# Six more out-weight blocks decoded during the attention, and GpSimd's forms set aside during the first left sums

## The chip, the core and the metric

The kernel runs on one core of a Trainium2 chip. The core has TensorE (PE in the profile; PEld are its weight loads), VectorE (DVE), ScalarE (ACT), GpSimd (POOL) and SyncE (SP), which issues nearly all DMAs. Each engine works through its own queue in order and waits for others by semaphores. The metric is the device time of one execution in microseconds (us). Everything is fp32 except the routing of the attention.

## The reference

Two stages follow each other. The first is attention with routing: 4 batches x 8 heads, 768 positions, 64 dimensions per head, 16 centroids per head. The second is a feed-forward block on the 3072 tokens x 512 features that come out.

```python
q_n = q / (norm(q) + 1e-6); k_n, c_n likewise
q_assign = argmax(einsum('bhsd,hcd->bhsc', q_n, c_n)); k_assign likewise
scores = where(q_assign[..., None] == k_assign[..., None, :], q @ k.T / 8, -1e9)
attn   = exp(scores - max); attn = attn / (sum + 1e-9)
x      = (attn @ v) -> (B*S, H*D) = (3072, 512)

h   = x @ w_in                      # w_in 512 x 2048
sp  = softplus(h)
out = (h * erf(sp)) @ w_out         # w_out 2048 x 512
```

## The kernel before

**Attention.** Two heads make a pair; there are 16 pairs (`NPAIR`), and each pair has 12 units of work: two halves of the queries by six blocks of keys. A period, `period(p, i)` (line 1343), handles two units; a pair has six periods, i = 0 to 5. In a period TensorE computes the scores of its two units into PSUM (`products`, `scores`), ScalarE takes the exponential (`curve`, written to the tiles `pr`), GpSimd adds the exponentials up (`accumulate`, line 548, 128x768, written to `more_out`) and TensorE multiplies those of the period before with v (`attend`). At i = 0 and i = 3 a half is complete: `divide` (line 573) begins with a TensorE product of the accumulated sum with a constant tile, `turned<-more_out,minus` in the profile; it needs GpSimd's last sum of the half. Half a pair ahead of all this, `maxima_step` (line 461) lets TensorE compute the scores once more, in bf16, into the PSUM tile `wide`, and VectorE takes their maxima (`nmx<-wide`). There is one `wide`: TensorE writes it again when VectorE has read it.

**Decoding the weights.** The products of the feed-forward block run by fast matrix multiplication of Strassen's kind. Each weight is read from DRAM as 64-bit numbers and made into fp32 on the chip, in 32 blocks of 128x512 values: blocks 0 to 15 are w_in, 16 to 31 w_out. For one block: `fetch` (a DMA of 512 KB into a place), `size`, `rest` and `sign` on ScalarE, `bounded` and `shifted` on VectorE (tensor_scalar), `summed` on GpSimd (int32, 128x512), after which the place is refetched for a later block. The first `N_EARLY` = 32 - `N_LATE` blocks are done inside the attention, two per pair: block n1 = 2p - 1 mostly in periods 1 to 4 of pair p, block n2 = 2p from period 3 of pair p to period 1 of pair p + 1. They use five places: two halves each of the token buffers `x_of[0]` and `x_of[1]`, and a part of `x_more`. With `N_LATE` = 10 these are blocks 0 to 21, and the last is finished in pair 11. Token chunk 0 is loaded into `x_of[0]` behind pair 11 (`load_x(0)`, `LAST_X`).

**Forms.** Fast multiplication needs sums and differences of matrix blocks. `left_forms` of the weights and `right_forms` of the first tokens are made in the last pairs: the list `forms` is taken from in turn by VectorE (`FORMS` says how many in which period of which pair, line 1409) and by GpSimd (in the pairs of `POOL_FORMS`, at `i % HJ == 1`, that is in periods 1 and 4, line 1436). On GpSimd a form stands in the queue behind the accumulations of its period's call.

**The first feed-forward stages.** Tokens are worked on in chunks of 512. `hidden(0, 0)` and `hidden(0, 1)` are the two halves of the hidden layer of chunk 0: 28 steps each, where a step is four matmul instructions into one of eight PSUM banks, followed by one or two VectorE operations that empty the bank (`block`, line 726; the bank of step k is used again by step k + 8). Between steps, `block` issues side work from the list `aside_work`, `pace` items per step. `gates` is such work: ScalarE's Softplus and Erf of a finished quarter (128x2048), an idle stretch in the list, four VectorE products with the result, and four left sums (`add_hidden`) for the next multiplication. `weights(n)` (line 1541) is the decoding of a late block in five items; its last item also lets GpSimd make `MADE_BEFORE[n]` of the 18 forms of `forms_twice` (line 969) whose results go to DRAM from `x_of[1]` and another tile. `out_forms` are GpSimd's forms of w_out, four per group. `project(0, 0)` is the first part of the output product; its side work needs token chunk 1, which is loaded into `x_of[1]` (line 1586).

All order is program order: `InOrder` (line 126) keeps each engine's instructions as the program issues them. Its line 136 is the line of nearly every instruction in the profile, so instructions are told apart by tiles.

Of the kernel before, what the change touches and what calls it, by code (L numbers as in the profile page):

```python
# [28 lines left out]
HJ = NJ // 2  # L29
# [8 lines left out]
LC = 512  # L38

UP = 2.0**16  # L40
PLACES = 5
FORMS = {12: {0: 1}, 13: {0: 1}, 14: {0: 1, 3: 1}, 15: {0: 1, 3: 2, 4: 2, 5: 2}}
POOL_FORMS = range(12, 16)
BIG = 2.0**60
FLOOR = 2.0**50
EPS = 2.0**-70
NPT = NJ + 2
N_LATE = 10
LAST_X = 11
MASKS = {(0, 2): ("k", 0), (2, 0): ("q", 0), (2, 2): ("k", 1), (5, 2): ("q", 1)}  # L50
FIRST_MASKS = {(2, 0): ("k", 0), (2, 1): ("q", 0), (2, 2): ("k", 1), (5, 2): ("q", 1)}
# [63 lines left out]
WHERE = {"x": (0, 0), "u": (0, 1), "w": (1, 1)}  # L115
TWICE = 2
BY_VECTOR = 4
MADE_BEFORE = (3, 3, 1, 1, 0, 1, 3, 2, 0, 0)
LAST_AT = (3, 6, 9, 12, 15, 18, 21)
EARLY_OUTERS = 6  # L120
STORE_AFTER = 2
# [23 lines left out]
def kernel(  # L145
# [145 lines left out]
    for f in range(HF):  # L291
        for g in (f, HF + f):
            w_steps.append((w_out[:, g], moe_w_out[g * P : (g + 1) * P]))
    N_EARLY = len(w_steps) - N_LATE

    x_of = {n: xp.tile([P, DM // P, CT], F32, name="x_own") for n in range(2)}
    places = [x_of[n][:, i : i + 2].rearrange("p k t -> p (k t)") for n in range(2) for i in (0, 2)]
    places.append(x_more.rearrange("p a k t -> p (a k t)")[:, 0 : 2 * LC])
    place_of = {n: places[n % PLACES] for n in range(N_EARLY)}
    after_of = {n: n + PLACES for n in range(N_EARLY - PLACES)}  # L300
    steps = {}

    def fetch(n):
        t = place_of[n]
        queues[0].dma_start(out=t.bitcast(U32), in_=w_steps[n][1])
        words = t.rearrange("p (n w) -> p n w", w=2)
        steps[n] = words[:, :, 1], words[:, :, 0], t.bitcast(I16)[:, 1 : 4 * LC : 4]
# [8 lines left out]
    def size_and_rest(n):  # L316
        size(n)
        rest(n)
# [360 lines left out]
    g_of = {}  # L679
    sums_of = {}  # L680
# [9 lines left out]
    aside_work = []  # L690
# [68 lines left out]
    def gate(n, lot, s):  # L759

        g = g_of[n, s, lot].rearrange("p h j t -> p (h j t)")
        box = []

        def curves():
            t = actp.tile([P, 2 * FG * HT], F32, name="a_s")
            box.append(t)
            ae.activation(out=t, in_=g, func=ACT.Softplus)
            ae.activation(out=t, in_=t, func=ACT.Erf)

        def product(i):  # L770
            c = slice(i * 512, (i + 1) * 512)
            ve.tensor_tensor(out=g[:, c], in0=box[0][:, c], in1=g[:, c], op=ALU.mult)

        return curves, [functools.partial(product, i) for i in range(2 * FG * HT // 512)]
# [5 lines left out]
    def idle(n):  # L780
        return [lambda: None] * n

    def gates(n, lot, which=(0, 1), between=()):
        work = list(between)
        for s in which:
            curves, products_of = gate(n, lot, s)
            if s == which[0]:
                work = [curves] + work + idle(7 - len(work)) + products_of
            else:
                work += [curves, *sums, *idle(3)] + products_of  # L790
            sums = add_hidden(n, lot, s)
        return work + sums
# [531 lines left out]
    def run(work):  # L1324
        for _ in work:
            pass
# [10 lines left out]
    forms = []  # L1337
# [5 lines left out]
    def period(p, i):  # L1343
        u = 2 * NJ * p + 2 * i
        n1, n2 = 2 * p - 1, 2 * p
        early = lambda n: 0 <= n < N_EARLY

        def mask(place):
            which = (MASKS if p else FIRST_MASKS).get((i, place))
            if which:  # L1350
                return masks(p + 1, *which, turned[0 if i in (0, 5) else 1], place > 1, ve if i == 0 else ae)
            return lambda: None

        if u > 0:
            for which in turns if i in (0, 3) else ():
                turn(*which)
                turns.remove(which)
            step_ahead(u)
        mask(0)()
        next(part[0], None)  # L1360
        if i == 5:
            next(routing[0], None)
        if i == 0 and p:
            run(routing[0])
        if u == 2:
            next(routing[0])
        products(u)
        products(u + 1)
        mask(1)()
        second = step_ahead(u + 1, True) if u > 0 else iter(())  # L1370
        next(second, None)
        rows = D if u == 0 or u + NJ >= len(units) else Q
        scores(u, rows)
        next(second, None)
        if i:
            next(second, None)
        next(part[0], None)
        scores(u + 1, rows)
        later = mask(2)
        if i == 0:  # L1380
            later()
            later = lambda: None
            next(second, None)
        if i == 3:
            similarities(p + 2)
            routing[0] = choose(p + 2, sc_of[u + 1][:, 0], True)
        curve(u)
        later()
        curve(u + 1)
        if u == 0:  # L1390
            step_ahead(1)
            similarities(1)
            routing[0] = choose(1, turned[0])
            next(routing[0])
            next(routing[0])
            vectors(1, "q")
            vectors(1, "k")
        if i == 0 and early(n1 - 1):
            bounded(n1 - 1)
            shifted(n1 - 1)  # L1400
            sign(n1 - 1)
        elif i == 1 and early(n1):
            size_and_rest(n1)
        elif i == 3 and early(n1):
            bounded(n1)
            sign(n1)
        elif i == 5 and early(n2):
            rest(n2)
        for _ in range(min(len(forms), FORMS.get(p, {}).get(i, 0))):
            forms.pop(0)[0]()  # L1410
        if i == 3:
            next(routing[0], None)
            if early(n1):
                shifted(n1)
            for _ in range(2):
                next(routing[0], None)
        elif i == 1:
            load(p + 1, "v", v, vp)
            if p == 0:
                run(routing[0])  # L1420
                transposes(2, "q")
        elif i == 2:
            transposes(p + 2, "k")
        elif i == 4:
            vectors(p + 2, "k")
            vectors(p + 2, "q")
        elif i == 5:
            transposes(p + 3, "q")
        if u > 0:
            if i == 1 and early(n1 - 1):  # L1430
                summed(n1 - 1)
            elif i == 4 and early(n1):
                summed(n1)
            for w in (u - 2, u - 1):
                accumulate(w)
            if i % HJ == 1 and p in POOL_FORMS and forms:
                forms.pop(0)[1]()
            for w in (u - 2, u - 1):
                attend(w)
            if i % HJ == 0:  # L1440
                part[0] = divide(u - 1)
                next(part[0])
        if i == 3 and early(n2):
            size(n2)
# [43 lines left out]
        copy()  # L1488
    transposes(1, "q")
    load(0, "v", v, vp)  # L1490
    for n in range(PLACES - 1):
        fetch(n)
    for i in range(NJ):
        run(maxima_step(0, i, also if i % 2 else wide))
# [6 lines left out]
    turn(0, 0, (ae.copy, ve.tensor_copy))  # L1501
    turns.clear()
    transposes(1, "k")
    fetch(PLACES - 1)
    queues[0] = queues[1] = sy
    for p in range(NPAIR):
        for i in range(HJ * 2):
# [25 lines left out]

    places = [gsp.tile([P, 3, FG, P], F32, name="g_more").rearrange("p a j t -> p (a j t)") for _ in range(2)]
    places += [outp.tile([P, 2, DM], F32, name="osb").rearrange("p h m -> p (h m)") for _ in range(2)]
    place_of.update({N_EARLY + i: places[i % 4][:, 0 : 2 * LC] for i in range(N_LATE)})
    after_of.update({N_EARLY + i: N_EARLY + i + 4 for i in range(N_LATE - 4)})
    for i in range(4):
        fetch(N_EARLY + i)

    def weights(n):
# [4 lines left out]
    making = forms_twice(  # L1546
        GROUPS[1][1][:EARLY_OUTERS],
        (actp.tile([P, 2 * FG * HT], F32, name="a_s"), x_of[1].rearrange("p k t -> p (k t)")),
    )
# [4 lines left out]
    def summed_after_forms(n):  # L1554
        for _ in range(MADE_BEFORE[n - N_EARLY]):
            next(making, idle(1)[0])()
        summed(n)

    def all_weights(lo, hi):
        return sum((weights(n) for n in range(lo, hi)), [])  # L1560

    out_forms = [right_forms(ge, *w_out_parts(f, 2)) for f in range(0, HF, 2)]

    def fence():
        t = up.tile([P, HM], F32, name="u")
        g = g_of[1, 0, 0][:, 0, 0, 0:1]
        ge.tensor_tensor(out=t[:, 0:1], in0=g, in1=g, op=ALU.add)

    def together(a, b):
        work = []  # L1570
        while a or b:
            work += a[:1] + b[:1]
            del a[:1], b[:1]
        return work
# [1 line left out]
    aside_work += idle(3) + all_weights(0, 4) + out_forms[0] + out_forms[1]  # L1576
    hidden(0, 0, {0: finish_attention})
    finish_aside()
    aside_work += together(idle(2) + gates(0, 0, (0,)), all_weights(4, N_LATE))
    hidden(0, 1, pace=2, first=ve.tensor_copy)  # L1580
    finish_aside()
    for store in making:
# [4 lines left out]
    aside_work += gates(0, 0, (1,)) + gates(0, 1, (0,), right_forms(ve, *x_parts(1)))  # L1587
    project(0, 0, 3)
    finish_aside()
    aside_work += together(gates(0, 1, (1,)), idle(2) + [fence] + out_forms[3])  # L1590
    take_places(2)
    hidden(1, 0, first=ve.tensor_copy)
    finish_aside()
# [1 line left out]
    making = forms26(EARLY_FORMS)  # L1595
# [7 lines left out]
    making = forms26(LATE_FORMS)  # L1603
# [41 lines left out]
```

## Time and profile before

| what | value |
|---|---|
| median of three runs | 967.66 us (966.88 to 968.11) |
| the profiled execution, its own time | 967.78 us |
| its span, first to last instruction | 966.1 us |
| attention, first exponential of pair 0 to the last `attend` | 20.2 to 407.4 us |
| `hidden(0, 0)`, TensorE | 407.41 to 432.27 us |
| `hidden(0, 1)`, TensorE | 432.27 to 463.95 us |
| `project(0, 0)`, TensorE | from 463.95 us |
| GpSimd busy, slices 2 to 16 of 40 | 8 or 9 tenths |
| granted TensorE clock, mean | 0.997 |

A line of the timeline gives the start in us from the span's start, the duration, the engine, the line, the operation, the tiles written and read, the shape, how many such instructions are merged in the line, and in brackets the idle time of the engine before it with what ended it. Ends of matmuls are modelled and overlap the next start, so the pace of TensorE is read from start to start. A digit of a slice is the busy share in tenths of a 24.15 us slice, which happens to be nearly one pair.

### The profile page before, as it was taken

Reading aid. Unit: us, or ns where it says so; the run is one execution under the profiler, and the core shown is the slowest. Engines: PE = TensorE matmul, PEld = TensorE weight load, DVE = VectorE, ACT = ScalarE, POOL = GpSimd, SP = SyncE. Lnnn points to the kernel's source line nnn. Section 1 sums busy time; section 2 is a strip of 40 time slices with the busy share of each in tenths; the row PEclk is TensorE's granted clock in tenths of the full one; section 3 lists DMA queues with packets and bytes.
Section 4 is the critical chain, followed back from the end, with each engine's and each line's share of the span. In section 5 each row is a group of like instructions: output and inputs, shape, how many; then the busy total and the mean of one; then the engine's idle time right before and its main releaser. Section 6 shows DMA issues by size and latency. Waiting matters only on the chain.

```text
span 966.1 us, 22439 instructions
## 1 busy us (share of the span) xinstructions
PE 953.0 (99%) x8954; PEld 729.1 (75%) x8954; DVE 810.8 (84%) x1399; ACT 540.8 (56%) x815; POOL 536.7 (56%) x370
## 2 busy tenths in 40 slices
PE   8999999999999999998999999999999999999998
PEld 3555555555555555686888888998999899989987
DVE  8888888888888876889779889788968987896887
ACT  3777777777777665467523542544266235625541
POOL 1688888888888888899369910360044015202700
PEclk9999999999999999999999999999999999999999
DMA  9355444444434311083203445363445336343533
GB/s 219 64 111 111 111 111 110 111 111 111 89 68 106 72 35 35 18 287 123 100 1 153 156 141 151 127 202 114 160 121 172 113 131 208 109 142 122 155 118 110
DMA packets 172313, 116.06 MB, mean 120 GB/s; under 512 B 131376, under 2 KB 141104, under 8 KB 172208
## 3 DMA queue, kind: packets, MB, share of 16 engines
q1 hardware_dynamic: 169280, 113.41, 42.1%
q8 instruction: 71, 1.16, 0.5%
q10 hardware_dynamic: 2928, 1.21, 0.4%
q14 instruction: 34, 0.28, 0.1%
HBM read 90.21 MB, written 24.38 MB: 119 GB/s over the span
## 4 chain that ended last, share of the span: by engine, by line
PE 93%; DVE 3%; DMA 1%; ACT 1%; issue 1%; SPq 0%; DVEq 0%; ACTq 0%
PE bank L136 40%; PE turned L136 31%; PE sc L136 17%; PE wide L136 6%; DVE g L136 1%; DVE w_out L136 1%; DVE nmx L136 1%; DMA out_dram<-osb 0%; ACT a_s L136 0%; DMA in_k<-in_k_dram 0%; DVE osb L136 0%; SPq L136 0%; DMA in_q<-in_q_dram 0%; DVE kT L136 0%; ACT g_more L136 0%
## 5 line engine op out<-in xcount | busy, mean ns | idle before, releaser
L136 POOL TENSOR_TENSOR more_out<-more_out,pr 128x768 f32<-128x768 f32 x128 | 217.1, 1696 | 18.7 <-ACT pr L136 10.1
L136 DVE TENSOR_REDUCE nmx<-wide 128x2 f32<-128x768 f32 x189 | 180.5, 955 | 47.4 <-PE wide L136 46.8
L136 ACT ACTIVATE pr<-sc 128x768 f32<-128x768 f32 x192 | 148.7, 810 | 94.0 <-PE wide L136 77.2
L136 POOL TENSOR_TENSOR g<-g 128x512 f32<-128x512 f32 x36 | 47.1, 1309 | 217.5 <-DVE g L136 215.6
L136 PE MATMUL turned<-pr,in_v 128*32 128x193 f32 x3072 | 144.8, 330 | 0.0
L136 PEld LDWEIGHTS turned<-pr,in_v 128*32 128x32 f32 x3072 | 91.6, 110 | 50.7 <-issue 21.3
L136 PE MATMUL sc<-qT,kT 64*128 64x384 f32 x528 | 98.4, 486 | 0.0
L136 DVE TENSOR_TENSOR g<-g 128x512 f32<-128x512 f32 x114 | 79.9, 700 | 16.4 <-PE bank L136 12.9
L136 DVE TENSOR_TENSOR g<-a_s,g 128x512 f32<-128x512 f32 x80 | 75.3, 966 | 4.2 <-ACT a_s L136 4.2
L136 POOL TENSOR_TENSOR more_out<-pr,pr 128x768 f32<-128x768 f32 x32 | 60.4, 1887 | 27.9 <-ACT pr L136 27.9
L136 PE MATMUL bank<-w_out,g 128*128 128x256 f32 x328 | 75.7, 380 | 0.0
L136 DVE TENSOR_TENSOR g<-bank,g 128x256 f32<-128x256 f32 (+1 forms) x129 | 63.7, 522 | 13.1 <-PE bank L136 5.9
L136 ACT ACTIVATE a_s<-g 128x1024 f32<-128x1024 f32 (+1 forms) x36 | 41.0, 1149 | 60.0 <-POOL g L136 45.6
L136 PE MATMUL bank<-x_own,w_in 128*128 128x128 f32 (+1 forms) x432 | 72.0, 309 | 2.3 <-DVE g L136 2.3
L136 PE MATMUL bank<-g_more,g 128*128 128x256 f32 x304 | 71.8, 379 | 0.0
L136 PEld LDWEIGHTS bank<-w_out,g 128*128 128x128 f32 x328 | 62.1, 190 | 9.6 <-issue 1.4
L136 PEld LDWEIGHTS <-qv 64*128 64x128 bf16 x384 | 26.9, 93 | 52.8 <-issue 36.7
L136 PEld LDWEIGHTS bank<-x_own,w_in 128*128 128x128 f32 x432 | 60.9, 192 | 7.0 <-DVE g L136 3.1
L136 PEld LDWEIGHTS sc<-qT,kT 64*128 64x128 f32 x528 | 49.6, 187 | 21.7 <-ACT inv L136 2.7
L136 PE MATMUL wide<-kv,qv 64*128 64x384 bf16 x378 | 64.0, 328 | 1.1 <-ACT km L136 0.6
L136 PEld LDWEIGHTS bank<-g_more,g 128*128 128x128 f32 x304 | 57.8, 190 | 7.8
L136 PE MATMUL wide<-km,qm 64*128 64x384 bf16 (+1 forms) x378 | 62.6, 327 | 0.0
(243 smaller groups left out, 2066.6 us busy)
## 6 DMA issues: line engine op xcount, KB each, us to landing
g_more<-b_dram SPq DMA_DIRECT2D x48, 512.0 KB, 3.6
g_more<-w_dram SPq DMA_DIRECT2D x84, 256.0 KB, 2.8
x_own<-in_moe_w_in_dram SPq DMA_DIRECT2D x13, 512.0 KB, 5.5
in_v<-in_v_dram SPq DMA_DIRECT2D x32, 192.0 KB, 3.1
x_dram<-more_out SPq DMA_DIRECT2D x128, 48.0 KB, 1.7
x_own<-x_dram SPq DMA_DIRECT2D x6, 1024.0 KB, 5.5
in_k<-in_k_dram SPq DMA_DIRECT2D x59, 96.0 KB, 2.7
in_q<-in_q_dram SPq DMA_DIRECT2D x58, 96.0 KB, 4.8
```

The source lines that it names most:

```text
L136: ins = getattr(self.engine, name)(*args, **kw)
```

## The change

- `N_LATE` goes from 10 to 4: blocks 22 to 27 (w_out) are decoded in the attention as well, in pairs 11 to 14. Their places follow `PLACE_OF`: blocks 0 to 24 go round the five places as before, and blocks 25, 26 and 27 use the two places in `x_of[1]`, where no token chunk is loaded yet.
- GpSimd's forms of the attention are taken in pairs 8 to 15, one per pair at period 4, instead of two per pair in pairs 12 to 15 at periods 1 and 4. Their number is the same, eight.
- In `hidden(0, 0)` the late blocks are now 28 to 31, and three forms of `forms_twice` stand between them instead of eight.
- In `hidden(0, 1)` the six blocks are gone from the side work. Since they were interleaved with the gate's items and the pace stays at two, the gate's items now go two to a step. Behind the four left sums GpSimd gets a one-column operation (`fence`) that reads the last of them; then come eight forms of `forms_twice`. Three more follow after the stage.

TensorE's order of instructions is the same.

```diff
-PLACES = 5
-POOL_FORMS = range(12, 16)
+POOL_FORMS = range(8, 16)
-N_LATE = 10
+N_LATE = 4
+PLACE_OF = [n % 5 for n in range(25)] + [2, 3, 2]
...
-MADE_BEFORE = (3, 3, 1, 1, 0, 1, 3, 2, 0, 0)
+MADE_BEFORE = (3, 0, 0, 0)
+MADE = (0, 8)
...
-    place_of = {n: places[n % PLACES] for n in range(N_EARLY)}
-    after_of = {n: n + PLACES for n in range(N_EARLY - PLACES)}
+    place_of = {n: places[p] for n, p in enumerate(PLACE_OF)}
+    after_of = {n: n + 1 + PLACE_OF[n + 1 :].index(p) for n, p in enumerate(PLACE_OF) if p in PLACE_OF[n + 1 :]}
...
-            if i % HJ == 1 and p in POOL_FORMS and forms:
+            if i == 4 and p in POOL_FORMS and forms:
                 forms.pop(0)[1]()
...
-    place_of.update({N_EARLY + i: places[i % 4][:, 0 : 2 * LC] for i in range(N_LATE)})
-    after_of.update({N_EARLY + i: N_EARLY + i + 4 for i in range(N_LATE - 4)})
-    for i in range(4):
+    place_of.update({N_EARLY + i: places[i][:, 0 : 2 * LC] for i in range(N_LATE)})
+    for i in range(N_LATE):
         fetch(N_EARLY + i)
...
-    def fence():
+    def fence(g):
         t = up.tile([P, HM], F32, name="u")
-        g = g_of[1, 0, 0][:, 0, 0, 0:1]
         ge.tensor_tensor(out=t[:, 0:1], in0=g, in1=g, op=ALU.add)
...
-    aside_work += together(idle(2) + gates(0, 0, (0,)), all_weights(4, N_LATE))
+    def make():
+        next(making, idle(1)[0])()
+
+    aside_work += (
+        together(idle(2) + gates(0, 0, (0,)), [make] * MADE[0])
+        + [lambda: fence(sums_of[0, 0, 0][:, 2, 0, 0:1])] + [make] * MADE[1]
+    )
     hidden(0, 1, pace=2, first=ve.tensor_copy)
...
-    aside_work += together(gates(0, 1, (1,)), idle(2) + [fence] + out_forms[3])
+    aside_work += together(gates(0, 1, (1,)), idle(2) + [lambda: fence(g_of[1, 0, 0][:, 0, 0, 0:1])] + out_forms[3])
```

More of the change, by code (lines that the diff above doesn't have):

```diff
@@ L1490 @@
     load(0, "v", v, vp)
-    for n in range(PLACES - 1):
+    for n in range(len(places) - 1):
         fetch(n)
@@ L1503 @@
     transposes(1, "k")
-    fetch(PLACES - 1)
+    fetch(len(places) - 1)
     queues[0] = queues[1] = sy
```

## The prediction

> **What bounds the kernel now.** I read the page first (busy shares, slices, the chain of waits), then windows and timelines around the two places that the change touches. The page:
>
> ```profile
> span 966.1 us, 22439 instructions
> PE 953.0 (99%) x8954; PEld 729.1 (75%) x8954; DVE 810.8 (84%) x1399; ACT 540.8 (56%) x815; POOL 536.7 (56%) x370
> PE   8999999999999999998999999999999999999998
> POOL 1688888888888888899369910360044015202700
> PE 93%; DVE 3%; DMA 1%; ACT 1%; issue 1%; SPq 0%; DVEq 0%; ACTq 0%
> ```
>
> TensorE sets the time: whatever stops it lengthens the run, whatever runs beside it is free. Almost the only stop after the start is in the stage that the change unloads, the second half of the hidden layer of token chunk 0, which TensorE enters at 432.27 us. Its timeline there:
>
> ```profile
> 453.27 1.13 PE L136 MATMUL bank<-x_own,w_in 128*128 128x256 f32 x4 [1.77 <-DVE g L136]
> 454.96 1.13 PE L136 MATMUL bank<-x_more,more_in 128*128 128x256 f32 x4 [0.56 <-DVE g L136]
> 456.65 1.13 PE L136 MATMUL bank<-x_own,w_in 128*128 128x256 f32 x4 [0.56 <-DVE g L136]
> 459.73 2.07 PE L136 MATMUL turned<-x_more,more_in 128*128 128x256 f32 x4 [1.95 <-DVE g L136]
> 461.60 1.66 PE L136 MATMUL turned<-x_own,more_in 128*128 128x256 f32 x4
> 463.09 1.03 PE L136 MATMUL bank<-x_more,w_in 128*128 128x256 f32 x4
> ```
>
> It waits for VectorE to empty a PSUM bank; eight banks go round, so step 22 waits for the eviction of step 14. VectorE was late for the reason in its own timeline: beside a busy GpSimd, an operation that lives in SBUF takes 1.44 to 1.50 us, and alone 0.41 to 0.67; evictions out of PSUM keep 0.41.
>
> ```profile
> 446.59 1.50 DVE L136 TENSOR_SCALAR w_out<-w_out 128x512 f32<-128x512 f32 x1
> 448.00 0.41 DVE L136 TENSOR_TENSOR g<-bank,g 128x256 f32<-128x256 f32 x1
> 448.34 1.44 DVE L136 TENSOR_TENSOR g<-a_s,g 128x512 f32<-128x512 f32 x1
> 459.60 0.67 DVE L136 TENSOR_TENSOR g_more<-g,g_more 128x512 f32<-128x512 f32 x1
> 460.86 0.41 DVE L136 TENSOR_SCALAR w_out<-w_out 128x512 uint32<-128x512 uint32 x1
> ```
>
> In the attention TensorE has no idle row from 24 us on. A pair takes 24.43 us with a block's decode in it (pairs 1 to 8) and 24.44 without (pair 12). So decoding alone is free there. What is not free is lateness at two places: GpSimd's last sum of a half, which the product with `minus` needs, and VectorE's first maximum of a pair's period 1, which empties `wide`.
>
> ```profile
> 280.00 1.30 POOL L136 TENSOR_TENSOR w_out<-w_out,x_more 128x512 int32<-128x512 int32 x1 [1.86 <-ACT x_more L136]
> 281.25 1.84 POOL L136 TENSOR_TENSOR more_out<-pr,pr 128x768 f32<-128x768 f32 x1
> 283.17 6.97 POOL L136 TENSOR_TENSOR more_out<-more_out,pr 128x768 f32<-128x768 f32 x4
> ...
> 290.92 0.51 PE L136 MATMUL turned<-more_out,minus 128*32 128x192 f32 x8
> ```
>
> ```profile
> 266.76 0.88 DVE L136 TENSOR_SCALAR w_out<-w_out 128x512 f32<-128x512 f32 x2
> 267.55 0.95 DVE L136 TENSOR_REDUCE nmx<-wide 128x2 f32<-128x768 f32 x1
> ...
> 268.56 0.34 PE L136 MATMUL wide<-kv,qv 64*128 64x384 bf16 x2
> ```
>
> The reader is to see a chain of GpSimd operations with no idle time in it, ending at 290.14, 0.78 us before its consumer; and a reduction that ends at 268.50, 0.06 us before TensorE writes the bank again: no room left.
>
> **Part 1, the stage that is unloaded (gain).** Six blocks leave it: 12 tensor_scalars of VectorE, 18 activations, 6 GpSimd sums and 6 fetches. 28 steps of four matmuls at 5.18/24 = 0.216 us are 24.2 us; the stage took 432.27 to 463.95, 31.7. So 7.5 us are to be had at most. With nothing interleaved, the gate's products now come five steps after its curves, and two work items a step go to them. I follow VectorE by these rows. The 2048-wide Softplus, table load and Erf took 1.91 + 1.28 + 1.91 us; started near 433 they end near 438.2, half a microsecond after VectorE gets there. GpSimd is then in its eight out-weight forms (eight took 11 us; from about 430 to 441). So the first two products cost 1.44 each, the other two and the four left sums 0.62 in cadence; with the evictions at 0.34 between them VectorE is through near 446. TensorE's step 16 would start at 446.1 and needs the eviction of step 8, done near 444.6; step 17, at 447.0, needs that of step 9, done near 446.2. It holds by less than 1 us. From there on VectorE has only evictions (0.34 each, about eight per 6.05 us of TensorE), and the eight resumed GpSimd forms do not slow those. Bounds: nothing is left of the stall (7.5 gained), or all eight operations are contended at 1.44, VectorE is at step 9 near 451.5 and TensorE loses 4.5 (3.0 gained). I take 7.3, near the first, since GpSimd's forms run out in the middle.
>
> The GpSimd forms that leave the first half of the hidden layer give VectorE air there, but TensorE has no idle row in that half: nothing.
>
> What is late next: eight plus three GpSimd forms, 1.38 us each, now run from 446 to 461, then the four of `out_forms[2]` to 466.5. Load of x chunk 1 waits for their stores: issued near 464, landed near 470 (its median is 5.5 to 6.1). VectorE wants that chunk 15.1 us into the projection (479.06 less 463.95), now at 471.6. Hidden, and eight banks of 1.73 us steps cover some us more. In the projection VectorE waits for Erf until 8.8 us anyway. Nothing.
>
> **Part 2, six more blocks in pairs 11 to 14.** Per pair two fetches, six activations, four tensor_scalars, two sums, as in pairs 1 to 10, whose length says nothing. SP's queue carries the fetches past the loads and stores as it did there; block 27 takes block 25's place three periods (12 us) ahead, landing 5.5. ScalarE goes from 15.0 to 19.1 busy of 24.4, as in pair 10. Nothing, but for what these meet in part 3.
>
> **Part 3, GpSimd's forms in pairs 8 to 15, now in period 4.** There each stands behind the first sum of the second half and ahead of the other four. In pair 14, where a form stood there already, the distance from the first sum to the second was 3.43 us (376.35 to 379.78, a wait of 0.38 in it) against 1.92 above: a form makes the chain 1.13 later. Before, no pair had both a block's sum and a form in that half; now pairs 8 to 14 have. Slack 0.78 (0.76 to 0.86 over all pairs); the smallest distance ever seen from sum to product is 0.05. So TensorE stops 1.13 - 0.78 + 0.05 = 0.40 in period 0 of each next pair. After pair 14 it is more: that pair has no similarities, its product comes 0.72 sooner while the sum still waits for ScalarE's sign, 1.1 in all.
>
> **Part 4, decode and form meet on VectorE** in period 0 of pairs 12, 13 and 14. Before, it had two tensor_scalars (0.79) or one form (0.68) between two maxima; now both. The next maximum comes 0.68 later, and the row above has no room: a stop of about 0.65, of which the 0.40 of part 3 is a part (TensorE's wait moves the need back), not an addition.
>
> Sum: pairs 9 to 11, 3 x 0.40 = 1.2; 12 to 14, 3 x 0.65 = 2.0; 15, 1.1: **4.3 lost**. Bounds: zero, if the stops are made up; upward each of four sums at 2.01, as they run beside VectorE's forms at 402.5 us, instead of 1.69: 1.3 more at seven places, 13 us lost. I take 4.3, since there VectorE's only neighbours are PSUM operations, as in the 1.69 rows.
>
> Does the stopping itself cost clock? After the stop of 1.95 us, eight matmuls took 1.67 us longer than their equals (2.07 and 1.66 against 1.03); after 0.56, 0.10 a group. Stops of 0.4 to 1.1: 0 to 0.9 in all; I take 0. [...]
>
> Total: -7.3 + 4.3 = -3.0. The profiled execution took 967.78, 1.7 beyond its span and 0.12 over the median of the three runs; 967.78 - 3.0 - 0.1 = **964.7**.
>
> **Rivals.** (a) The attention absorbs it: the stops of parts 3 and 4 do not appear, 967.7 - 7.3 = 960.4. For it: the pair's length never moved with its load. Against it: the slacks above. 0.17. (b) The stage stays late: GpSimd's forms reach into two of the left sums, VectorE is at step 9 near 449.8, TensorE loses 2.8, gain 4.7, with 4.3 lost: 967.3, no change. For it: less than 1 us of room. 0.13. (c) Slower: GpSimd's chain of sums in pairs 8 to 14 is drawn out by VectorE's transposes and tensor_scalars. It decides from a loss of 7.3, that is 1.04 at each of seven boundaries; at 8 to 10 the time is 968.4 to 970.4, and at the price of the 2.01 rows, 13, it is 973. For it: one form in pair 12 made such a sum 2.35 instead of 1.81. Against: the sums of all pairs keep 1.69. 0.20. That the blocks do not move is no rival: the order of instructions has them in pairs 11 to 14 and TensorE's order unchanged. The forecast has 0.50, by itself 963 to 966.3.
>
> **How the numbers follow.** 0.2% is 1.9 us, about what a measurement of this kernel can tell: faster means below 965.7. (a) and nearly all of the forecast are faster: 0.17 + 0.46 = 0.63. Same: 0.04 of the forecast, (b), a little of (c): 0.19. Slower: 0.18. The range takes in (a) and the lower end of (c): 960.2 to 969.
>
> **What would show it.** After: no idle TensorE rows for `g` in the stage, its last matmul about 24.5 us after its first, VectorE's products 1.4, 1.4, then 0.7. In the attention pairs 9 to 11 last 24.8, 12 and 13 about 25.1, and the 1.1 falls in pair 15 (a pair taken from its first exponential to the next pair's); before each `minus` product that opens a pair, GpSimd's chain ends 0.05 earlier, and in pairs 12 to 14 `nmx` starts right behind the form. Wrong if pairs keep 24.4, or if `nmx` of a later period is late too.

## The result and the profile after

The changed kernel takes **964.06 us** (median of six runs, 963.70 to 964.65), the kernel before on the same chip 967.72 us (six runs, 966.88 to 969.46). The ratio is 0.9962, its 95% interval 0.9949 to 0.9975: faster by 0.4%. 964.7 was forecast. The profiled execution took 963.70 us with a span of 962.0; before it was 967.78 and 966.1.

The page after, with the span, the busy shares, GpSimd's slices and the chain of waits:

```profile
span 962.0 us, 22444 instructions
PE 951.8 (99%) x8954; PEld 727.4 (76%) x8954; DVE 798.2 (83%) x1399; ACT 538.9 (56%) x815; POOL 531.4 (55%) x371
POOL 1688888888888888887479910360054016202600
PE 96%; DVE 2%; DMA 1%; POOL 0%; issue 0%; ACT 0%; SPq 0%; DVEq 0%; POOLq 0%
```

TensorE's share of the chain goes from 93 to 96%. Its timeline in the unloaded stage, `hidden(0, 1)`, has no idle row. The stage opens at 436.45 and the projection, whose first row reads `w_out`, at 460.62. The first lines here are the opening, the last ones the end:

```profile
436.45 1.03 PE L137 MATMUL bank<-x_own,w_in 128*128 128x256 f32 x4
437.31 1.03 PE L137 MATMUL turned<-x_own,w_in 128*128 128x256 f32 x4
...
451.12 1.03 PE L137 MATMUL turned<-x_own,w_in 128*128 128x256 f32 x4
...
459.76 1.03 PE L137 MATMUL bank<-x_more,w_in 128*128 128x256 f32 x4
460.62 1.67 PE L137 MATMUL bank<-w_out,g 128*128 128x256 f32 x7
```

That is 24.17 us where it was 31.61 from the same row to the same row (432.34 to 463.95), a gain of 7.4. VectorE and GpSimd in the middle of the stage show why:

```profile
443.60 1.29 DVE L137 TENSOR_TENSOR g<-a_s,g 128x512 f32<-128x512 f32 x2 [1.35 <-ACT a_s L137]
445.14 1.29 DVE L137 TENSOR_TENSOR g<-a_s,g 128x512 f32<-128x512 f32 x2
446.68 0.68 DVE L137 TENSOR_TENSOR g_more<-g 128x512 f32<-128x512 f32 x1
...
449.54 0.95 DVE L137 TENSOR_TENSOR g<-turned,g 128x256 f32<-128x256 f32 x2
...
442.40 1.28 POOL L137 TENSOR_TENSOR more_out<-more_out,w_out 128x512 f32<-128x512 f32 x1
449.70 0.19 POOL L137 TENSOR_TENSOR u<-g_more 128x1 f32<-128x1 f32 x1 [6.03 <-DVE g_more L137]
449.85 1.27 POOL L137 TENSOR_TENSOR x_own<-more_in,x_own 128x512 f32<-128x512 f32 x1
```

GpSimd's last form before the pause ends at 443.68; its one-column fence waits 6.03 us for VectorE's last left sum. In between VectorE has four products and four sums, at 0.61 to 0.69 us each. Step 9 is emptied by the first of the two operations from 449.54 on, near 449.95, 1.2 us before step 17 (451.12) needs its bank.

In the attention the stops are there. A pair, from its first exponential to the next pair's, took 24.43 to 24.45 before in pairs 1 to 8 and does so after; then (pair 9 contains 0.16 that it had before as well):

| pair | 9 | 10 | 11 | 12 | 13 | 14 | first period of 15 |
|---|---|---|---|---|---|---|---|
| period 0 before, us | 4.09 | 4.09 | 4.09 | 4.06 | 4.06 | 4.06 | 4.06 |
| period 0 after, us | 4.46 | 4.47 | 4.44 | 4.69 | 4.69 | 4.69 | 5.12 |
| pair after, us | 24.97 | 24.81 | 24.79 | 25.04 | 25.04 | 24.33 | |

The timeline after, first GpSimd's and TensorE's in the last boundary (into pair 15), then GpSimd's, TensorE's and VectorE's in the boundary into pair 12:

```profile
381.87 1.84 POOL L137 TENSOR_TENSOR more_out<-pr,pr 128x768 f32<-128x768 f32 x1
383.66 1.28 POOL L137 TENSOR_TENSOR w_in<-w_in 128x512 f32<-128x512 f32 x1
384.88 6.97 POOL L137 TENSOR_TENSOR more_out<-more_out,pr 128x768 f32<-128x768 f32 x4
391.90 0.53 PE L137 MATMUL turned<-more_out,minus 128*32 128x192 f32 x8 [0.85 <-POOL more_out L137]
...
309.83 6.98 POOL L137 TENSOR_TENSOR more_out<-more_out,pr 128x768 f32<-128x768 f32 x4
316.86 0.53 PE L137 MATMUL turned<-more_out,minus 128*32 128x192 f32 x8 [0.21 <-POOL more_out L137]
316.75 0.88 DVE L137 TENSOR_SCALAR w_out<-w_out 128x512 f32<-128x512 f32 x2
317.54 0.69 DVE L137 TENSOR_TENSOR more_in<-w_in 128x512 f32<-128x512 f32 x1
318.14 0.95 DVE L137 TENSOR_REDUCE nmx<-wide 128x2 f32<-128x768 f32 x1
```

The four sums end at 391.85 and 316.81, each 0.05 us before the product with `minus`, which TensorE waited for; before, they ended 0.76 to 0.86 earlier. The form of 1.28 us stands between the first sum and the other four. And in the boundary into pair 12 the maximum follows the form at once. Matching TensorE's matmuls one by one in the two traces, after falls 4.1 us behind over these seven boundaries, is 3.3 us ahead when the projection begins, and 4.1 ahead at the end of the trace.

### The profile page after: what moved, and what is told of

Its sections match the earlier page's. It is cut to its first block, busy times and chain, and to the rows that moved or that the text cites. A ratio compares the mean times of both kernels' runs of the same rounds, so it can differ in the third digit from the quotient of the medians.

```text
span 962.0 us, 22444 instructions
## 1 busy us (share of the span) xinstructions
PE 951.8 (99%) x8954; PEld 727.4 (76%) x8954; DVE 798.2 (83%) x1399; ACT 538.9 (56%) x815; POOL 531.4 (55%) x371
## 4 chain that ended last, share of the span: by engine, by line
PE 96%; DVE 2%; DMA 1%; POOL 0%; issue 0%; ACT 0%; SPq 0%; DVEq 0%; POOLq 0%
PE bank L137 42%; PE turned L137 31%; PE sc L137 17%; PE wide L137 6%; DVE nmx L137 1%; DVE km L137 0%; POOL more_out L137 0%; DMA in_k<-in_k_dram 0%; SPq L137 0%; DMA in_q<-in_q_dram 0%; DVE kT L137 0%; ACT qm L137 0%; DVE sims L137 0%; DVE qT L137 0%; ACT pr L137 0%
## 5 line engine op out<-in xcount | busy, mean ns | idle before, releaser
L137 DVE TENSOR_TENSOR g<-a_s,g 128x512 f32<-128x512 f32 x80 | 72.4, 932 | 5.6 <-ACT a_s L137 5.6
```

The lines of the kernel that those rows point to most:

```text
L137: ins = getattr(self.engine, name)(*args, **kw)
```

## The experiments

Each run had the kernel before beside it on the same chip, and each kernel was timed five to eleven times. Not all runs share a chip (the median of before lies between 967.50 and 968.15), so ratios are taken against before on the run's own chip, and steps of less than 1 us between runs are read from the traces. "After" stands for the changed kernel.

| run | what is different | median, us (range) |
|---|---|---|
| after | | 964.06 (963.70 to 964.65) |
| e4_no_pause | after without the pause | 972.54 (972.15 to 973.03) |
| e5_pause_only | before with a pause | 964.47 (963.92 to 964.64) |
| e8_forms_only | before with the new place of GpSimd's forms | 969.54 (968.23 to 971.05) |
| e2_forms_to_gpsimd | after, VectorE's forms of pairs 12, 13 on GpSimd | 964.15 (964.05 to 964.50) |
| e1_sum_first | after, first sum of the second half ahead of the block's sum | 968.66 (968.54 to 969.39) |
| e3_both | e1 and e2 together | 966.80 (966.41 to 966.99) |
| e6_form_in_gap | after, GpSimd's forms at period 0 | 961.49 (961.10 to 961.85) |
| e7_form_behind_decode | e6 with the forms held back | 970.44 (970.32 to 970.97) |
| e9_last_stop | e6 with one form moved | 960.85 (960.60 to 960.91) |

### e4_no_pause: is the stage's gain owed to the pause?

```diff
         together(idle(2) + gates(0, 0, (0,)), [make] * MADE[0])
-        + [lambda: fence(sums_of[0, 0, 0][:, 2, 0, 0:1])] + [make] * MADE[1]
+        + [make] * MADE[1]
```

> The changed kernel without the one-column operation that makes GpSimd wait for the left sums: its eight forms follow the out-weight forms without a pause, at 443.6 us instead of 449.9. Theory: the four left sums (446.7 to 449.6) then take 1.43 instead of 0.68, VectorE reaches the eviction of step 9 some 3 us later (452.5), step 17 of TensorE wants it at 451.15, so TensorE stops by 1 to 2 us: 965.3 (964.5 to 966.3). Rival: the decode's departure alone makes the stage fit, the pause is for nothing, 964.0 to 964.3; or faster, since the forms end 6 us earlier and token chunk 1 with them.

Measured 972.54 us, 8.5 more than after. The attention is as in after; the stage alone takes 8.5 us more, longer than it took before the change. GpSimd's forms follow on at 445.28, and this is the timeline of VectorE and TensorE:

```profile
444.21 3.32 DVE L137 TENSOR_TENSOR g<-a_s,g 128x512 f32<-128x512 f32 x2 [1.35 <-ACT a_s L137]
447.79 3.09 DVE L137 TENSOR_TENSOR g<-a_s,g 128x512 f32<-128x512 f32 x2
451.14 1.42 DVE L137 TENSOR_TENSOR g_more<-g 128x512 f32<-128x512 f32 x1
455.81 1.75 DVE L137 TENSOR_TENSOR g_more<-g,g_more 128x512 f32<-128x512 f32 x1
...
445.28 1.71 POOL L137 TENSOR_TENSOR x_own<-more_in,x_own 128x512 f32<-128x512 f32 x1
...
451.27 1.13 PE L137 MATMUL bank<-x_own,w_in 128*128 128x256 f32 x4 [1.10 <-DVE g L137]
454.61 1.25 PE L137 MATMUL bank<-x_more,more_in 128*128 128x256 f32 x4 [2.21 <-DVE g L137]
457.95 2.08 PE L137 MATMUL turned<-x_own,w_in 128*128 128x256 f32 x4 [2.08 <-DVE g L137]
459.82 1.91 PE L137 MATMUL turned<-x_more,more_in 128*128 128x256 f32 x4
461.52 1.42 PE L137 MATMUL bank<-x_own,more_in 128*128 128x256 f32 x4
```

Products and sums of two SBUF operands take 1.4 to 1.75 us each instead of 0.61 to 0.69, GpSimd's forms 1.59 to 1.71 instead of 1.27. A group of four matmuls takes 0.865 us from start to start; the group ahead of each stop and the stop now take 2.13 (449.14 to 451.27), 3.34 and 3.34, and the three groups behind the last stop 1.87, 1.70 and 1.26. That is 6.2 us of waiting and 2.2 of slower matmuls, together the 8.5. The windows of the trace give the granted clock over these 13 us, behind the busy times (0.74):

```profile
451.00:464.00 13.00, 8.44 (x26) 6.36 (x27) 11.64 (x20) 0.00 (x0) 12.53 (x10) 0.74 0.45 177
```

The direction was as expected, the size was not: the expectation counted the four left sums, and in the run all eight operations and the clock pay. The first product's share is not the missing pause's: it ran from 444.21 beside the last out-weight form, which ended 8.3 us into the stage (445.32 less 437.06) and 7.2 in after; one trace does not say how often that happens. So the blocks' departure makes no gain without the pause: the forms that the departed sums leave room for run into the gate.

### e5_pause_only: the pause without the unloading

Before, with the late blocks in their places; six of the forms of `forms_twice` wait behind the last left sum:

```diff
-MADE_BEFORE = (3, 3, 1, 1, 0, 1, 3, 2, 0, 0)
+MADE_BEFORE = (3, 3, 1, 1, 0, 0, 0, 0, 0, 0)
+MADE = 6
...
-    aside_work += together(idle(2) + gates(0, 0, (0,)), all_weights(4, N_LATE))
+    aside_work += together(
+        idle(2) + gates(0, 0, (0,)) + [lambda: fence(sums_of[0, 0, 0][:, 2, 0, 0:1])] + [make] * MADE,
+        all_weights(4, N_LATE),
+    )
```

> The kernel before, with the pause alone: all ten late blocks stay behind the attention and GpSimd's forms of the attention stay in pairs 12 to 15, but in the second half of the hidden layer the six forms that stood between the blocks wait, as in the changed kernel, for the last left sum. Theory (what makes that stage late is VectorE's operations meeting GpSimd's forms, and not their number): nine operations of 1.43 to 1.50 us between 446.6 and 459.3 shrink to 0.34 to 0.62 in cadence, some 7 us; the stage loses 0 to 2 us instead of 7.5 and the attention nothing: 961.7 (960.3 to 963.5), below the changed kernel. Rival (the six blocks have to leave, the pause is the smaller part): 965 to 967.

Measured 964.47 us; ratio 0.9965, interval 0.9952 to 0.9977. That is 2.8 us above the expected time and 1.0 above the upper end given, but it is as good as the whole change. TensorE's idle rows in the stage that are above 0.2 us, and then its rows in the projection, with VectorE's:

```profile
453.25 1.13 PE L137 MATMUL bank<-x_more,more_in 128*128 128x256 f32 x4 [0.47 <-DVE g L137]
458.16 1.13 PE L137 MATMUL bank<-x_more,w_in 128*128 128x256 f32 x4 [0.31 <-DVE g L137]
...
474.21 1.13 PE L137 MATMUL bank<-w_out,g 128*128 128x256 f32 x4 [0.25 <-DVE g L137]
476.62 1.99 PE L137 MATMUL bank<-more_out,g_more 128*128 128x256 f32 x8 [1.28 <-DVE g_more L137]
...
469.39 4.77 DVE L137 TENSOR_TENSOR g<-a_s,g 128x512 f32<-128x512 f32 x3
474.75 1.09 DVE L137 TENSOR_TENSOR g_more<-g 128x512 f32<-128x512 f32 x1
```

The attention is that of before (pairs of 24.43). Counting from the beginning of the work, the projection opens 5.2 us earlier than before; then 2.1 are lost there, because the GpSimd work that was held back now runs beside the projection's products (1.59 us each). So the pause brings about 5 of the 7.4 us, and the unloading the rest and the freedom of the projection, for which it pays 4.1 in the attention. As the change was made, the two halves cancel.

### e8_forms_only: are the stops owed to the forms or to the decoding?

Before, and nothing but `POOL_FORMS` and the period of after:

```diff
-POOL_FORMS = range(12, 16)
+POOL_FORMS = range(8, 16)
...
-            if i % HJ == 1 and p in POOL_FORMS and forms:
+            if i == 4 and p in POOL_FORMS and forms:
```

> The kernel before, with the change's new place of GpSimd's forms alone (pairs 8 to 15, period 4); blocks, pause and stage as before. Theory: a stop of 0.37 to 0.40 us at the minus product that opens pairs 9 to 12, where a form stands behind a block's sum in the half before (pairs 8 to 11), none behind pairs 12 to 14, which have no block to sum: 967.72 + 1.5 = 969.2 (968.7 to 969.8). Rival: without more blocks in the attention nothing stops, 967.5 to 968.

Measured 969.54 us; ratio 1.0016, interval 1.0007 to 1.0025. Period 0 of pairs 9 to 12 takes 4.49, 4.47, 4.46 and 4.49; of pairs 13 to 15 it takes 4.06. So a stop of 0.4 needs both a form and a block's sum in the half before it: in pairs 8 to 11 blocks were decoded in this kernel too, in pairs 12 to 14 not, and there the form costs nothing. These four make +1.6 in the trace. The profiled execution, with 969.3 of span, has a further 1.7 us in `hidden(0, 1)` and at the start of the projection, whose work is that of before. The stops there are those of before (0.2 us more in all); the matmuls behind them are slower for longer:

```profile
461.91 2.07 PE L136 MATMUL turned<-x_more,more_in 128*128 128x256 f32 x4 [1.95 <-DVE g L136]
463.77 1.91 PE L136 MATMUL turned<-x_own,more_in 128*128 128x256 f32 x4
465.48 1.91 PE L136 MATMUL bank<-x_more,w_in 128*128 128x256 f32 x4
467.19 4.07 PE L136 MATMUL bank<-w_out,g 128*128 128x256 f32 x16
```

These three groups take 1.86, 1.71 and 1.71 us from start to start and the 16 matmuls 3.91; in before, behind the same stop of 1.95, it was 1.87, 1.49, 0.86 and 3.46. The granted clock over the 12 us from that stop on is 0.74, in before 0.87. The wide spread of the runs goes with the clock: four of the eleven have a mean of 0.996 and take 970.5 to 971.1 us, the others 0.997 or 0.998 and 968.2 to 969.7. Why the clock comes back later in some executions is open.

### e2_forms_to_gpsimd: does the decode meet the form on VectorE?

```diff
-FORMS = {12: {0: 1}, 13: {0: 1}, 14: {0: 1, 3: 1}, 15: {0: 1, 3: 2, 4: 2, 5: 2}}
-POOL_FORMS = range(8, 16)
+FORMS = {14: {3: 1}, 15: {0: 1, 3: 2, 4: 2, 5: 2}}
+POOL_FORMS = range(6, 16)
...
-            if i == 4 and p in POOL_FORMS and forms:
+            if (i == 4 and p in POOL_FORMS or (p, i) == (15, 1)) and forms:
```

> The changed kernel, with VectorE's forms of period 0 in pairs 12, 13 and 14 taken away; GpSimd makes three more forms instead, in period 4 of pairs 6 and 7 and in period 1 of pair 15. Theory (VectorE is late in period 0 of pairs 12 to 14 because of two tensor_scalars and a form between two maxima, beside GpSimd's lateness): pairs 12 and 13 fall from 25.04 to about 24.8, pair 14 by 0.23, but pairs 7 and 8 rise to 24.8, since GpSimd's chain now has a form behind a sum there too: 964.06 - 0.7 + 0.8 = 964.1 (963.5 to 964.7). Rival (more work as such): the load has only moved to earlier pairs, which shows nothing in their length, 963.3 or less.

Measured 964.15 us, as expected. Without VectorE's form, period 0 of pairs 12, 13 and 14 falls from 4.69 to 4.49, 4.35 and 4.46, the price of GpSimd's chain alone; in exchange pairs 7 and 8 stop too (4.46, 4.47). The two stops of a boundary overlap, as the prediction had it: 0.60 with both, 0.4 with GpSimd's alone.

### e1_sum_first and e3_both: the first sum ahead of the block's sum

If the chain of GpSimd is what is late, its first sum should not stand behind the decoded block's sum, which waits for ScalarE's sign. Here it goes first, the block's sum and the form follow, then the other four. For this the second tensor_scalar was moved forward too:

```diff
         elif i == 3 and early(n1):
             bounded(n1)
+            shifted(n1)
             sign(n1)
...
-            if early(n1):
-                shifted(n1)
...
-            elif i == 4 and early(n1):
-                summed(n1)
             for w in (u - 2, u - 1):
                 accumulate(w)
+            if i == 4 and early(n1):
+                summed(n1)
```

> The changed kernel, with one reordering in period 4 of every pair: GpSimd's first accumulation of the second half stands ahead of the decode's sum and of the form (it can start when the exponentials of period 3 are there, about 1.3 us before ScalarE's sign lets the sum start), and VectorE's second tensor_scalar of that block stands directly behind the first, so that it is done before that accumulation takes its turn. All work is kept. Theory (GpSimd's chain of sums is late, 0.37 us a pair in pairs 9 to 11 and 1.06 in pair 15): the chain ends some 0.9 us before the minus product again, pairs 9 to 11 last 24.4 (24.8 to 25.0 in the changed kernel), pair 15's first period 4.1 instead of 5.1, and pairs 12 to 14 keep their 0.6, since there VectorE is as late: 964.06 - 2.1 = 962.0 (961.4 to 962.6). Rival (the attention is longer because VectorE, ScalarE and GpSimd have more work in it, in whatever order): no pair changes, 964 to 964.3. Second rival: the earlier accumulation holds VectorE's tensor_scalars up, the maximum of period 4 comes late in every pair, slower than 965.

Measured 968.66 us; ratio 1.001, interval 1.0002 to 1.0019. Where the edit aims, it does what it should: GpSimd's chain ends 0.85 us before the product at every boundary, period 0 of pairs 9 to 11 is 4.09 again and of pair 15 it is 4.06; pairs 12 to 14 keep 4.69, VectorE's part. But period 3 of pairs 1 to 13 now lasts 5.16 instead of 4.76 and of pair 14 5.60 instead of 4.06. The timeline in pair 4:

```profile
132.82 0.88 DVE L137 TENSOR_SCALAR w_in<-w_in 128x512 f32<-128x512 f32 x2
133.62 0.58 DVE L137 STREAM_TRANSPOSE sims<-turned 128x384 f32<-128x384 f32 x1
134.34 0.53 PE L137 MATMUL turned<-more_out,minus 128*32 128x192 f32 x8 [0.25 <-DVE sims L137]
```

In after, one tensor_scalar of 0.42 stands there, the transpose to `sims` runs from 131.58 to 132.16 and the product starts at 132.34 with no wait. `minus` writes a bank that the transpose reads. So 13 x 0.40 + 1.54 = 6.7 us were lost and 2.2 won (1.1 in pairs 9 to 11, 1.06 in pair 15), +4.5; measured +4.6. The second tensor_scalar had a place with about 0.2 us of room on a wait that the prediction did not list at all.

> The changed kernel with both edits: the first accumulation ahead of the sum and the form in period 4, and no VectorE form in period 0 of pairs 12 to 14 (GpSimd makes three more). Theory: all stops of TensorE in the attention go, every pair lasts 24.4 and pair 15's first period 4.1; 964.06 - 4.1 = 960.0 (959.4 to 961.0), below both kernels. Rival (more work as such): 963.5 to 964.3.

Both edits together: 966.80 us; ratio 0.9991, interval 0.9982 to 0.9999. All stops of period 0 are gone (4.09 in every pair, 4.06 in pair 15), the loss in period 3 is the same. Against e1 it gained 1.9, which is three times the 0.60 of VectorE's forms.

### e6_form_in_gap: the form at period 0

The stops come from a form in the second half, where the block's sum also is. At period 0 GpSimd has no block's sum ahead of it. Here its forms go there, and VectorE's forms of pairs 12 to 14 go to GpSimd as well.

```diff
-FORMS = {12: {0: 1}, 13: {0: 1}, 14: {0: 1, 3: 1}, 15: {0: 1, 3: 2, 4: 2, 5: 2}}
-POOL_FORMS = range(8, 16)
+FORMS = {14: {3: 1}, 15: {0: 1, 3: 2, 4: 2, 5: 2}}
+POOL_FORMS = range(7, 16)
...
-            if i == 4 and p in POOL_FORMS and forms:
+            if (i == 0 and p in POOL_FORMS or p == 15 and i in (1, 4)) and forms:
```

> The changed kernel, with GpSimd's forms in period 0 of pairs 7 to 15 (and two more in periods 1 and 4 of pair 15), behind the last accumulation of a half, where GpSimd waits 2.3 us for ScalarE's sign; no VectorE form in period 0 of pairs 12 to 14. Theory: no chain of sums is late any more, but the form runs from about 0.8 us ahead of the minus product to 0.45 us behind its start, and VectorE's first tensor_scalar waits 0.1 to 0.3 us for it: pairs 7 to 14 last 24.5 to 24.75, pair 15's first period 4.1: 964.06 - 4.1 + 8 x 0.17 = 961.4 (960.4 to 962.6). Rival (more work as such): 963.5 to 964.5.

Measured **961.49 us**; ratio 0.9935, interval 0.9922 to 0.9947: below both kernels. Pairs 7 to 14 last 24.48, 24.49, 24.63, 24.48, 24.46, 24.62, 24.43 and 23.78, pair 15's first period 4.06. One stop is left, where pair 15 has two forms in one half; its period 3 lasts 4.52 instead of 3.62:

```profile
400.92 0.53 PE L137 MATMUL turned<-more_out,minus 128*32 128x192 f32 x8 [0.75 <-POOL more_out L137]
```

### e7_form_behind_decode: what a longer first half costs

e6 has VectorE's tensor_scalars of period 0 and GpSimd's form side by side. To take them apart, in pairs 7 to 14 GpSimd first reads one column of the block that VectorE has just shifted:

```diff
+                if i == 0 and early(n1 - 1):
+                    w = w_steps[n1 - 1][0].bitcast(I32)[:, 0:1]
+                    ge.tensor_tensor(out=hold, in0=w, in1=w, op=ALU.add)
                 forms.pop(0)[1]()
```

> As the run before, but in pairs 7 to 14 a one-column GpSimd operation that reads the block's shifted values makes the form wait for VectorE's two tensor_scalars of period 0; the block's sum then comes some 0.9 us later, in a half whose chain had 0.95 us of slack. Theory: neither the tensor_scalars nor the minus products wait, every pair lasts 24.4 to 24.5: 964.06 - 4.0 = 960.1 (959.6 to 961.2). Rival (more work as such): 963.5 to 964.5.

Measured 970.44 us; ratio 1.0029, interval 1.0017 to 1.004. Period 0 is 4.09 everywhere, as meant, but period 3 of pairs 7 to 13 lasts 5.86 instead of 4.76 (5.69 in pair 9) and of pair 14 4.92 instead of 4.06: 8.4 us together. Matched with e6, the attention is 7.8 us longer, against 9.0 measured (970.44 less 961.49). The other 1.2 lie ahead of it: the first exponential starts at 21.65 us, in e6 at 20.48; whether that belongs to the edit is open. The timeline in pair 8:

```profile
221.31 0.19 POOL L137 TENSOR_TENSOR hold<-w_in 128x1 int32<-128x1 int32 x1 [2.10 <-DVE w_in L137]
225.85 6.97 POOL L137 TENSOR_TENSOR more_out<-more_out,pr 128x768 f32<-128x768 f32 x4
231.59 1.51 DVE L137 TENSOR_SCALAR w_in<-w_in 128x512 f32<-128x512 f32 x1
233.03 0.57 DVE L137 STREAM_TRANSPOSE sims<-turned 128x384 f32<-128x384 f32 x1
233.75 0.53 PE L137 MATMUL turned<-more_out,minus 128*32 128x192 f32 x8 [0.88 <-DVE sims L137]
```

GpSimd waits 2.10 us, and its last sum now ends at 232.82. VectorE's tensor_scalar of period 3, 0.42 in after, starts inside that sum and takes 1.51, until 233.10; the transpose and the product follow. The tensor_scalar ends 0.28 us after the sum does, not at some stretched rate of its own; what holds it until then no view shows. In before, sixteen tensor_scalars of 128x512 between 407 and 470 us start inside a GpSimd operation; they take up to 1.50 us, and fifteen of them end 0.28 or 0.29 us after it.

### e9_last_stop: the last stop of e6

```diff
-FORMS = {14: {3: 1}, 15: {0: 1, 3: 2, 4: 2, 5: 2}}
+FORMS = {14: {3: 1, 5: 1}, 15: {0: 1, 3: 2, 4: 2, 5: 2}}
...
-            if (i == 0 and p in POOL_FORMS or p == 15 and i in (1, 4)) and forms:
+            if (i == 0 and p in POOL_FORMS or (p, i) == (15, 4)) and forms:
```

> This is e6 with one GpSimd form less in the last pair: the one of period 1 of pair 15 goes to VectorE in period 5 of pair 14, where VectorE has no decoding. If the one stop left in e6 (0.75 us before the product with minus in period 3 of pair 15) comes from two forms in one half, GpSimd's chain of that half ends in time again: period 3 of pair 15 returns from 4.52 to about 3.7 and the time falls by 0.75 to 0.9, to about 960.7. Rival: VectorE's form in period 5 of pair 14 makes the next maximum late there, as two tensor_scalars and a form did in period 0 of pairs 12 to 14; then that period grows by up to 0.6 and the time stays at 961.2 to 961.5. Second rival: the stop in pair 15 is owed to ScalarE's sign or to VectorE, not to the number of forms; then it stays at 0.75.

Measured **960.85 us** (five runs, 960.60 to 960.91); ratio 0.993, interval 0.9916 to 0.9944: the lowest median of all. The interval overlaps that of e6, so the step from e6 is read from the traces. Period 3 of pair 15 is back at 3.62, so two forms in a half were the cause. Of those 0.90 us 0.29 were given back: the first period of pair 15 takes 4.35, for a reason that neither rival named: VectorE's form in period 5 of pair 14 runs beside GpSimd's sums and draws them out. The timeline of e6 and then of e9, pair 14:

```profile
381.66 6.95 POOL L137 TENSOR_TENSOR more_out<-more_out,pr 128x768 f32<-128x768 f32 x4
```

```profile
381.69 7.29 POOL L137 TENSOR_TENSOR more_out<-more_out,pr 128x768 f32<-128x768 f32 x4
384.59 1.09 DVE L137 TENSOR_TENSOR more_in<-more_in,w_in 128x512 f32<-128x512 f32 x1
```

Of the 4.1 us that the change lost in the attention, 0.9 is left in this kernel; the stage gains 7.4 as in after.

## Why the prediction was right

**The stage.** -7.3 was forecast and -7.4 came (the prediction's 31.7 us counts from 432.27, where the first row of the stage is at 432.34). The path to it was not quite as described. The gate's curves ended later than forecast: Erf ended 7.1 us into the stage (443.56 less 436.45), forecast was about 5.9 (438.2 less 432.27). The forecast counted one table load, between the curves; a second one of 1.28 us stands ahead of Softplus, after ScalarE's wait for VectorE (437.14). GpSimd's eight forms ended 7.2 us in, forecast about 8.7 (441). So the products met practically no form, and took 0.61 to 0.69 us where two were to take 1.44. The two errors offset each other, which was luck: VectorE was through at 13.2 us (449.6 less 436.45), forecast 13.7 (446). The room before step 17, "less than 1 us", was 1.2. e4 shows how much hung on it: with GpSimd in the same 6 us, the stage takes 8.5 us more. Rival (b) had this mechanism for two of the left sums, at 2.8 us; it did not come, and with all eight operations hit it costs three times that. For that case the prediction's lower bound had 4.5 lost. It was too small: it took 1.44 an operation, where e4 has up to 1.75 and 6.2 us of waiting, and nothing for the clock, which cost 2.2.

**What is late next.** x chunk 1 was issued in two halves, at 464.7 and 467.2, which took 5.8 to 6.9 us; VectorE read it at 475.73 without a wait. Hidden, as forecast.

**Six more blocks.** They cost little: in e6, with the blocks in place and the forms at period 0, pairs 12 to 14 last 24.62, 24.43 and 23.78; before they lasted 24.44, 24.34 and 23.70. That is 0.35 together, where nothing was forecast, and a part of it belongs to the forms, which cost 0.05 a pair in pairs 7 and 8. No run has the six blocks alone.

**GpSimd's chain.** 0.40 was forecast for pairs 9 to 11 and 0.37, 0.38 and 0.35 came; 1.1 for pair 15, and 1.06 came. The 0.05 us between the last sum and the product stood as forecast. Rival (a), that the attention absorbs it all, did not come. e1 and e3, which let the first sum run before the block's sum, remove exactly these stops, and e8 makes them without the six blocks where both a form and a block's sum share a half. That settles the cause. Rival (c), sums drawn out to 2.01 us, did not come: the four sums take 6.97 as before.

**Decode and form on VectorE.** 0.65 was forecast and 0.63 came (4.69 less 4.06), `nmx` right behind the form. e2 removes VectorE's form and leaves 0.3 to 0.4, e3 removes both and leaves nothing.

**The clock.** 0 was taken, with 0.9 possible. The stops of 0.35 to 1.06 add to 4.0 us, and the lag at the end of the attention is 4.1: behind single stops no matmul was measurably slower than its equals (behind the longest, of 0.85 us at 391.90, the eight scores took 1.45 in after as in before, and the granted clock from 391 to 397 us was 1.00).

**What was not forecast.** The rest of the run, after the projection, is 0.7 us shorter in the trace of after than in the trace of before: TensorE in before was idle there for 0.31 at 701.34, waiting for ScalarE's `osb`, and no other trace has such a row. e8, whose feed-forward part is that of before, is 0.4 shorter there as well. So it isn't owed to the change, and why one execution has it is open. The sum of terms is -7.4 + 4.1 = -3.3; the medians have -3.7 and the spans, with these 0.7, -4.1.

The reading was incomplete in one respect: the prediction listed two places where lateness costs in the attention. e1 and e7 found a third, VectorE's transpose of the similarities in period 3, with 0.2 us of room. The change did not touch it, so the number stood; that the missing place did no harm was luck.

## What to carry to other kernels

A share of busy time does not say whether work fits beside a full engine; the distance from the end of a chain to its consumer does, and it must be read for every consumer, in each period. Work that moves to unload one stage goes best where nothing else stands ahead of the same chain: with the forms in the half that also has a block's sum the attention lost 4.1 us, with them at the start of the other half 0.9. Two engines that slow each other, as VectorE's products and sums of SBUF operands and GpSimd's forms did in e4 (1.4 to 1.75 us against 0.61 to 0.69, and 1.59 to 1.71 against 1.27), may be set one after the other by a wait on one column, but only where the held-back work has room later: taking the pause out of the one stage lost 8.5 us, and a like wait put into the attention lost 7.8 there.

## What the hardware showed

VectorE's products and sums of SBUF operands, 0.61 to 0.69 us each in after, took 1.4 to 1.75 beside running GpSimd forms in e4, and the forms themselves took between 1.59 and 1.71 instead of 1.27, while evictions out of PSUM kept 0.41 (e4). Of the sixteen tensor_scalars of before that start inside a GpSimd operation between 407 and 470 us, fifteen end 0.28 or 0.29 us after it, whether they take 0.63 us or 1.50; the one of 1.51 in e7 ends 0.28 after its sum. In e4 stops followed each other closely and the matmuls behind them were slower: after idle times of 1.10, 2.21 and 2.08 us within 8 us the next groups took 2.08, 1.91 and 1.42 instead of 1.03, at the granted clock of 0.74, while in after seven single stops up to 0.85 us, 24 us apart, cost nothing beyond themselves (clock 1.00 in the 5 to 7 us behind each). The price is not fixed: behind the same stop of 1.95 us the slower matmuls cost 1.6 us in the trace of before and 3.1 in that of e8.
